# A third landing buffer for weight pieces in a fused attention and two-layer MLP kernel, paid for with one buffer of normalised outputs and one of early transposed halves

## The chip, the core and the metric

One core of a Trainium2 chip runs the whole program. Its engines are named as the profile names them: PE (TensorE, with its weight loads PEld), DVE (VectorE), ACT (ScalarE), POOL (GpSimd) and SP (SyncE, which here issues nearly all DMAs; its rows are marked SPq). The metric is the device time of one execution in microseconds, the median of several runs.

## What is computed

Two batches of eight heads of clustered attention (768 positions, head size 64), then two pairs of dense layers on the 1536 tokens:

```
q_n, k_n, c_n = normalised q, k, centroids
q_assign = argmax(q_n @ c_n.T)          # 16 clusters per head
k_assign = argmax(k_n @ c_n.T)
mask = q_assign[..., :, None] == k_assign[..., None, :]
scores = where(mask, q @ k.T / sqrt(64), -1e9)
attn = softmax(scores)                  # + 1e-9 in the sum
x = (attn @ v) as [1536, 512]
x = softplus(x @ w_in1) @ w_out1        # 512 -> 2048 -> 512
out = leaky_relu(x @ w_in2, 0.01) @ w_out2
```

## The kernel before

**Numbers.** Every float32 operand of a product is split into two float16 halves, a high part and the rest, so that a product costs three matmuls of halves. The weights lie in memory in float64, as pairs of 32-bit integers: DVE puts a float32 together from each pair with three integer operations (`decode`, lines 140, 143 and 146), ACT scales and rounds it to the high half (line 162), DVE writes the low half (line 163).

**A piece of weights.** `w_piece` (line 150) handles 128 rows of 512 numbers. It takes a tile `st` of 4 KB per partition from the pool `wst`, which has two buffers of it, issues its load on SP (line 153), and returns a function `conv` that decodes and splits the piece later. There are 32 such pieces, 16 of `w_in1` and 16 of `w_out1`; here they are called piece 0 to piece 31. `w_step` (in the main function) converts the piece loaded in the step before and loads the next one. The load is put on SP behind the transpose `tq` of a head two ahead of the one at work (`behind_tk`, with `wtie["h"]`), so SP's queue holds head h+2's `tq` first and then the pieces of head h. All 32 pieces are converted while the attention runs. The weights of the last two layers come later by functions of their own, which also take `st` from `wst`.

**A head of attention.** For each of the 16 heads in turn: `split` casts q and k to halves (ACT lines 293 and 295 into `nq` and `n1`, POOL line 294) and transposes `n1` by DMA into `t` (line 297, pool tag `t1`: the early halves, of which the scores are made). `assign_mm` (PE line 306) and `assign_el` (DVE lines 319 to 325, ACT lines 328 and 329) find the clusters and write them beside the halves in `nq`; this is transposed into `tq` (line 331). `emit_s1` (PE line 345, DVE line 352) computes scores once for the row maxima, `emit_m` (PE line 366, ACT line 374) writes the maxima into `tq`, `emit_s2` (PE lines 392 and 393, ACT line 399) computes the scores again and their exponentials, `emit_pv` (PE lines 415 to 433) multiplies with v, `emit_empty` (PE line 451) closes the sum, and `emit_norm` divides (DVE line 473 into `y`) and splits the result (ACT line 475, POOL line 476).

**Buffers.** `BUFS` gives for each tag a pair (late, early): buffers in the pool `at`, which lives through the attention, and further ones in `ep`, used by the first eight heads alone and given back at head 8. Before, `t1` has (4, 2) and `y` has (2, 0). A head's `t` is free again after its last matmul of line 393.

**What sets the order.** The program is written with a priority on each step (`at_pri`), and a scheduler places all instructions engine by engine, by priorities and by its own estimate of times; each engine then runs its own list strictly in that order, SP too. A wait at the head of an engine's list therefore holds everything behind it. From head 8 on, steps of the first dense layer (`layer_in`, PE line 697, 16 steps of 12 matmuls; its activation is on ACT lines 520 to 523) are mixed in, then steps of the second (`layer_mid`, PE line 710).

Of the kernel before, what the change touches and what calls it, by code (L numbers as in the profile page):

```python
# [11 lines left out]
I32 = mybir.dt.int32  # L12
# [10 lines left out]


BUFS = {
# [4 lines left out]
}  # L30
N_BUFS, V_BUFS = (2, 2), 3
PSUM_BUFS = {"as": 1, "s1": 2, "s2": 2}
# [11 lines left out]

FF_PRI, FF_STEP, FF_RATE = 8, 0.25, 0.75

W_FREE, W_FROM, W_TO, W_PER = 4, 8, 10, 5
W_PRI = ((0, 0.5), (17, 0.3))
W2_STEPS = 88
# [7 lines left out]
def attn_moe_kernel(  # L57
# [27 lines left out]
    wst = ctx.enter_context(tc.tile_pool(name="wst", bufs=2, side="right"))  # L85
# [6 lines left out]
    at = bctx.enter_context(tc.tile_pool(name="at", bufs=1, side="right", reuse_waits="tile"))  # L92
# [3 lines left out]
    turn = {}  # L96
# [41 lines left out]
    def decode(c, st):  # L138
        lo, hi = st[:, :, 0], st[:, :, 1]
        V.tensor_scalar(  # L140
            out=c, in0=hi, scalar1=3, scalar2=0x3FFFFFFF, op0=ALU.logical_shift_left, op1=ALU.bitwise_and
        )
        V.scalar_tensor_tensor(  # L143
            out=c, in0=hi, scalar=-0x40000000, in1=c, op0=ALU.bitwise_and, op1=ALU.bitwise_or
        )
        V.scalar_tensor_tensor(  # L146
            out=c, in0=lo, scalar=29, in1=c, op0=ALU.logical_shift_right, op1=ALU.bitwise_or
        )
        return c

    def w_piece(dsth, dstl, src):
        st = wst.tile([128, 512, 2], I32, tag="st", name="st")
        nc.sync.dma_start(out=st, in_=src.rearrange("p (n t) -> p n t", t=2))

        def conv(bank=False):
            if bank:
                c = pm.tile([128, 512], I32, tag="m0", name="wcp")
            else:
                c = wst.tile([128, 512], I32, tag="wc", name="wc")
            decode(c, st)  # L160
            cf = c.bitcast(F32)
            S.activation(out=dsth, in_=cf, func=AF.Copy, scale=WS)
            V.scalar_tensor_tensor(out=dstl, in0=cf, scalar=WS, in1=dsth, op0=ALU.mult, op1=ALU.subtract)

        return conv

    def in_pieces(w, wh, wl):
        wi = w.bitcast(I32)
        for f in range(DFF // 512):
            for kk in range(KDM):  # L170
                cs = slice(f * 512, (f + 1) * 512)
                src = wi[kk * 128:(kk + 1) * 128, f * 1024:(f + 1) * 1024]
                yield partial(w_piece, wh[:, kk, cs], wl[:, kk, cs], src)

    def out_pieces(w, wh, wl):
        wi = w.bitcast(I32)
        for kk in range(KFF):
            yield partial(w_piece, wh[:, kk, :], wl[:, kk, :], wi[kk * 128:(kk + 1) * 128, :])
# [738 lines left out]
    st = {"credit": 0.0}  # L917
# [83 lines left out]
```

## Time and profile before

| | us |
|---|---|
| median of 3 runs | 734.42 (733.02 to 736.55) |
| profiled execution | 732.15 |
| its span | 730.4 |
| PE busy in the span | 677.0 (93%) |
| DVE busy | 517.3 (71%) |
| ACT busy | 410.9 (56%) |
| POOL busy | 402.5 (55%) |

The attention takes the first 274 us and a little more; its last head ends inside the second dense layer. Busy time of PE is modelled at each instruction's end: matmuls overlap, so a busy share says that PE had matmuls in flight and not that it could take no more. What PE lost is read from idle times and from the distance between starts. DMA-issuing instructions are shown on SP from the moment they are issued; the time before, when SP waits for a buffer, is in the view of waits.

### The profile page before, as it was taken

How to read it: one execution, taken by the hardware profiler on the slowest of the kernel's cores; microseconds unless marked ns; L12 is line 12 of the kernel's file. 1: busy time of each engine (PE TensorE's matmuls, PEld its weight loads, DVE VectorE, ACT ScalarE, POOL GpSimd, SP SyncE). 2: the span in 40 equal slices, each digit the busy share in tenths (PEclk: the TensorE clock that was granted, in tenths of full speed). 3: DMA queues.
4: the chain of work that ended last, by engine and by line, in shares of the span. 5: the costliest groups of instructions: out<-in, count | busy, mean ns of one | idle time of the engine just before them, and what ended most of it. 6: DMA issues, size and time to landing. Idle time of an engine off the chain costs nothing. (4 is left out here: it accounts for less than half of the span.)

```text
span 730.4 us, 18968 instructions
## 1 busy us (share of the span) xinstructions
PE 677.0 (93%) x7584; PEld 506.7 (69%) x7584; DVE 517.3 (71%) x1167; ACT 410.9 (56%) x1087; POOL 402.5 (55%) x494
## 2 busy tenths in 40 slices
PE   1798899998889899999999999999999999999997
PEld 1367677665656566656666566558999999999996
DVE  4797798998898782069787867965585757575545
ACT  5476666768878753355245425526555555565553
POOL 6387777778888864303324233325556465565653
PEclk9999999999999999999999999999999999999999
DMA  8985966766565632013322355787000000000000
GB/s 204 221 173 113 181 136 122 170 123 173 129 161 152 141 116 53 2 35 103 110 93 82 108 175 193 235 304 261 3 31 2 30 2 7 27 2 31 2 31 30
DMA packets 104521, 77.87 MB, mean 107 GB/s; under 512 B 78320, under 2 KB 92656, under 8 KB 104432
## 3 DMA queue, kind: packets, MB, share of 16 engines
q1 hardware_dynamic: 104288, 76.40, 40.4%
q8 instruction: 59, 0.97, 0.5%
q14 instruction: 30, 0.25, 0.1%
q10 hardware_dynamic: 144, 0.26, 0.1%
HBM read 50.36 MB, written 10.49 MB: 83 GB/s over the span
## 5 line engine op out<-in xcount | busy, mean ns | idle before, releaser
L401 POOL TENSOR_TENSOR pl<-p 128x768 f16<-128x768 f32 x88 | 128.3, 1468 | 56.3 <-ACT p L399 36.0
L352 DVE TENSOR_REDUCE mm<-s 128x1 f32<-128x384 f32 x190 | 100.6, 548 | 19.3 <-PE s L345 16.7
L562 PEld LDWEIGHTS <-w_in2h 128*128 128x128 f16 x1344 | 98.2, 98 | 5.3 <-issue 0.7
L570 DVE TENSOR_TENSOR gl<-r,gh 128x384 f16<-128x384 f32 (+1 forms) x96 | 63.2, 659 | 50.0 <-ACT gh L608 49.3
L697 PE MATMUL m<-xt,w_inh 128*128 128x384 f16 x512 | 93.8, 326 | 4.2 <-ACT rl L521 3.4
L399 ACT ACTIVATE p<-s 128x384 f32<-128x384 f32 x160 | 74.2, 492 | 30.9 <-PE s L393 28.3
L710 PE MATMUL m<-g_l,w_outh 128*128 128x384 f16 x256 | 83.4, 326 | 2.0 <-DVE g_l L511 1.9
L710 PE MATMUL m<-g_h,w_outh 128*128 128x384 f16 x256 | 83.5, 326 | 0.0
L710 PE MATMUL m<-g_h,w_outl 128*128 128x384 f16 x256 | 83.3, 326 | 0.0
L570 POOL TENSOR_TENSOR r<-r,r 128x128 f32<-128x128 f32 x95 | 47.8, 520 | 55.5 <-ACT r L600 55.2
L697 PEld LDWEIGHTS <-w_inh 128*128 128x128 f16 x512 | 49.7, 98 | 38.7 <-issue 6.1
L608 ACT CAST gh<-r 128x384 f16<-128x384 f32 (+1 forms) x96 | 54.2, 565 | 36.6 <-POOL r L570 33.6
L710 PEld LDWEIGHTS <-w_outh 128*128 128x128 f16 x512 | 49.8, 98 | 32.5
L345 PE MATMUL s<-tq 128*128 128x384 f16 x190 | 62.0, 345 | 9.3 <-DMA tq<-nq 4.5
L562 PEld LDWEIGHTS <-gh 128*128 128x128 f16 x672 | 60.5, 98 | 6.4 <-issue 1.1
L200 POOL TENSOR_TENSOR wd<-wd 128x256 f32<-128x256 f32 x32 | 29.3, 925 | 53.9 <-DVE sg L194 39.2
L562 PE MATMUL i<-xt,w_in2h 128*128 128x128 f16 x576 | 57.2, 219 | 0.1
L392 PE MATMUL s<-t 128*128 128x384 f16 x160 | 53.2, 333 | 3.1 <-ACT p L399 2.3
L393 PE MATMUL s<-tq 128*128 128x384 f16 x160 | 53.2, 333 | 1.6 <-ACT tq L374 1.6
L562 PE MATMUL i<-sh,w_in2h 128*128 128x128 f16 x384 | 53.5, 219 | 0.4 <-ACT r L600 0.4
L562 PE MATMUL i<-sl,w_in2h 128*128 128x128 f16 x384 | 53.5, 219 | 0.0
L562 PE MATMUL i<-sh,w_in2l 128*128 128x128 f16 x384 | 53.4, 219 | 0.0
(145 smaller groups left out, 1861.1 us busy)
## 6 DMA issues: line engine op xcount, KB each, us to landing
st<-in_moe_w_in_dram SPq DMA_DIRECT2D x32, 512.0 KB, 4.6
st<-in_moe_w_out_dram SPq DMA_DIRECT2D x32, 512.0 KB, 3.7
kept<-sg SPq DMA_DIRECT2D x16, 256.0 KB, 2.8
qk<-in_q_dram SPq DMA_DIRECT2D x16, 192.0 KB, 3.5
qk<-in_k_dram SPq DMA_DIRECT2D x16, 192.0 KB, 3.7
v<-in_v_dram SPq DMA_DIRECT2D x16, 192.0 KB, 4.7
kept<-sg SPq DMA_DIRECT2D x24, 128.0 KB, 2.7
out_dram<-ob SPq DMA_DIRECT2D x11, 256.0 KB, 2.0
```

Of the source, the lines that this page charges most:

```text
L200: G.tensor_tensor(out=out, in0=in0, in1=in1, op=ALU.subtract)
L345: PE.matmul(out=o, lhsT=t[:, c, :], rhs=tk[:, 3 * j:3 * j + 3, :], start=True, stop=True,)
L352: V.reduce_max(out=mms[h % 2][:, c, j:j + 1], in_=bank[:, 0:3 * 128], axis=AX)
L392: PE.matmul(out=o, lhsT=t1[:, kt, 1, :], rhs=t1[:, 3 * j:3 * j + 3, 0, :], start=True, stop=False)
L393: PE.matmul(out=o, lhsT=t2[:, kt, :], rhs=tqh[:, 3 * j:3 * j + 3, :], start=False, stop=True)
L399: S.activation(out=p[:, j, :], in_=sp, func=AF.Exp, scale=scale)
L401: G.tensor_tensor(out=pl, in0=p, in1=pb, op=ALU.subtract)
L562: one = PE.matmul(out=bank, lhsT=w_, rhs=x_, start=(first and i == 0), stop=(i == len(ops) - 1), skip_group_check=True)
L570: eng.tensor_tensor(out=out, in0=in0, in1=in1, op=op)
L608: S.copy(out=gh[:, lo:hi], in_=r[:, lo:hi])
L697: PE.matmul(out=hp, lhsT=w_, rhs=x_, start=(i == 0), stop=(i == len(ops) - 1))
L710: PE.matmul(out=yp, lhsT=w_[:, kk, ms], rhs=g_[:, kk, :], start=(n == 0), stop=(n == 3 * KFF - 1))
```

## The change

`w_piece` takes its tile in turn from three buffers: two of `wst`, and a third with the same tag in the pool `at`, so it exists in the attention alone. The turn counts pieces, so each piece's tile follows from its number. To make room, `y` goes from two buffers to one, and the early part of `t1` from two to one. The late part stays at four. Nothing is computed differently.

```diff
-    "qk": (2, 1), "n1": (1, 2), "t1": (4, 2), "tq": (3, 1),
+    "qk": (2, 1), "n1": (1, 2), "t1": (4, 1), "tq": (3, 1),
...
-    "dd": (2, 0), "y": (2, 0), "xn": (2, 0),
+    "dd": (2, 0), "y": (1, 0), "xn": (2, 0),
...
+ST_MORE = 1
...
     def w_piece(dsth, dstl, src):
-        st = wst.tile([128, 512, 2], I32, tag="st", name="st")
+        n = turn["st"] = (turn.get("st", -1) + 1) % (2 + ST_MORE)
+        st = (wst if n < 2 else at).tile([128, 512, 2], I32, tag="st", name="st", bufs=2 if n < 2 else ST_MORE)
         nc.sync.dma_start(out=st, in_=src.rearrange("p (n t) -> p n t", t=2))
```

The numbers of instructions stay the same on every engine; the scheduler puts many of them elsewhere. Lines from 152 on stand two lower in the changed kernel, so line 297 there is 299. Three places matter below.

On SP, early in the attention: `t_1261`, `t_1561` and `t_1861` are the early halves of heads 5, 6 and 7, `nq_85` is the `tq` transpose of head 4, `st` a piece of weights. Before:

```order
L274 DMA qk<-in_k_dram 128x384
L297 DMA_TRANSPOSE t_1561<-n_1554 128x12x128
L273 DMA qk<-in_q_dram 128x384
L274 DMA qk<-in_k_dram 128x384
L297 DMA_TRANSPOSE t_1861<-n_1854 128x12x128
L331 DMA_TRANSPOSE tq<-nq_85 128x12x128
L153 DMA st<-in_moe_w_in_dram 128x1024
L280 DMA v_1_93<-in_v_dram 128x6x64
L273 DMA qk<-in_q_dram 128x384
L274 DMA qk<-in_k_dram 128x384
L331 DMA_TRANSPOSE tq<-nq_86 128x12x128
L153 DMA st<-in_moe_w_in_dram 128x1024
```

After:

```order
L299 DMA_TRANSPOSE t_1261<-n_1254 128x12x128
L275 DMA qk<-in_q_dram 128x384
L276 DMA qk<-in_k_dram 128x384
L299 DMA_TRANSPOSE t_1561<-n_1554 128x12x128
L333 DMA_TRANSPOSE tq<-nq_85 128x12x128
L155 DMA st<-in_moe_w_in_dram 128x1024
L282 DMA v_1_93<-in_v_dram 128x6x64
L275 DMA qk<-in_q_dram 128x384
L276 DMA qk<-in_k_dram 128x384
L299 DMA_TRANSPOSE t_1861<-n_1854 128x12x128
L333 DMA_TRANSPOSE tq<-nq_86 128x12x128
L155 DMA st<-in_moe_w_in_dram 128x1024
```

The early halves stand later among the `tq` transposes: head 7's now stands directly ahead of the `tq` of head 5 (`nq_86`), while the piece of weights stays directly behind its `tq`.

On SP, some 30 us later: `t_2469` is the early halves of head 9, `nq_88` and the following `nq_85` are the `tq` transposes of heads 7 and 8. Before:

```order
L297 DMA_TRANSPOSE t_2469<-n_2462 128x12x128
L331 DMA_TRANSPOSE tq<-nq_88 128x12x128
L153 DMA st<-in_moe_w_in_dram 128x1024
L280 DMA v_1_93<-in_v_dram 128x6x64
L454 DMA_TRANSPOSE xt_83<-xn 128x12x128
L153 DMA st<-in_moe_w_in_dram 128x1024
L331 DMA_TRANSPOSE tq<-nq_85 128x12x128
```

After:

```order
L333 DMA_TRANSPOSE tq<-nq_88 128x12x128
L155 DMA st<-in_moe_w_in_dram 128x1024 x2
L282 DMA v_1_93<-in_v_dram 128x6x64
L456 DMA_TRANSPOSE xt_83<-xn 128x12x128
L299 DMA_TRANSPOSE t_2469<-n_2462 128x12x128
L333 DMA_TRANSPOSE tq<-nq_85 128x12x128
```

Head 9's halves moved from ahead of head 7's `tq` to directly ahead of head 8's, and one piece of weights moved up by two places.

On PE, where the closing sum of head 12 has freed a `tq` buffer and the first scores of head 15 wait for its `tq`: behind the last scores before the dense layer's step, before:

```order
L393 LDWEIGHTS tq
L393 MATMUL s_5113<-tq 128x384
L697 LDWEIGHTS w_inh
L697 MATMUL m<-xt_83,w_inh 128x384
L697 LDWEIGHTS w_inh
L697 MATMUL m<-xt_83,w_inh 128x384
```

After:

```order
L395 MATMUL s_5113<-tq 128x384
L712 LDWEIGHTS w_outh
L712 MATMUL m<-g_h,w_outh 128x384
L712 LDWEIGHTS w_outh
L712 MATMUL m<-g_l,w_outh 128x384
L712 LDWEIGHTS w_outl
```

Before, 12 matmuls of line 697 follow here and then 17 small ones of `emit_pv`; now 23 of line 710 (712 there) and 6 small ones.

## Rows read from the trace of the kernel before

**Rows 1.** Busy by stretch: stretch, us, each engine's busy us, PE clock, DMA share, GB/s

```profile
37.00:150.00 113.00, 104.28 (x1547) 77.92 (x1545) 96.23 (x230) 77.71 (x192) 86.73 (x72) 1.00 0.74 152
150.00:274.00 124.00, 110.17 (x1361) 74.22 (x1360) 105.62 (x217) 93.59 (x227) 97.88 (x87) 0.99 0.58 140
```

**Rows 2.** Timeline of PE: start us, us, line, operation, [idle before, releaser]; back-to-back matmuls

```profile
41.89 0.19 PE L429 MATMUL x<-v,p 128*128 128x64 f16 x1
41.92 0.19 PE L428 MATMUL x<-v,p 128*128 128x65 f16 x1
...
47.66 0.32 PE L392 MATMUL m<-t 128*128 128x384 f16 x1
47.82 0.32 PE L345 MATMUL s<-tq 128*128 128x384 f16 x1
```

**Rows 3.** Waits of SP: line, releaser, us in total, times, longest us

```profile
SPq L153 <- DVE wcp L146: 35.0, 10, 5.6
```

**Rows 4.** Waits of DVE for pieces, whole run, and two of them in the timeline

```profile
DVE wcp L140 <- DMA st<-in_moe_w_in_dram: 7.2, 3, 3.2
...
61.79 0.69 DVE L140 TENSOR_SCALAR wcp<-st 128x512 int32<-128x512 int32 x1 [3.25 <-DMA st<-in_moe_w_in_dram]
...
166.97 0.69 DVE L140 TENSOR_SCALAR wcp<-st 128x512 int32<-128x512 int32 x1 [1.68 <-DMA st<-in_moe_w_in_dram]
```

**Rows 5.** Timeline of SP, the loads of those two pieces

```profile
55.23 1.50 SPq L331 DMA_TRANSPOSE tq<-nq  x1
56.82 0.86 SPq L153 DMA_DIRECT2D st<-in_moe_w_in_dram  x1
...
161.83 1.45 SPq L153 DMA_DIRECT2D st<-in_moe_w_in_dram  x2
```

**Rows 6.** Timeline of POOL and DVE, two heads' normalised outputs

```profile
55.68 0.92 POOL L476 TENSOR_TENSOR xn<-y,xn 128x384 f16<-128x384 f32 x1
...
66.33 0.56 DVE L473 TENSOR_TENSOR y<-x,dd 128x384 f32<-128x384 f32 x1
```

**Rows 7.** Timeline of ACT, SP and PE around the tq of head 5

```profile
70.09 0.27 ACT L329 ACTIVATE nq<-oh 128x96 f16<-128x96 f16 x1
...
70.38 1.46 SPq L331 DMA_TRANSPOSE tq<-nq  x1
...
71.43 0.33 PE L393 MATMUL m<-tq 128*128 128x384 f16 x1
...
75.43 0.92 ACT L293 CAST nq<-qk 128x384 f16<-128x384 f32 x2 [2.80 <-DMA tq<-nq]
...
76.90 0.32 PE L393 MATMUL m<-tq 128*128 128x384 f16 x1 [1.77 <-ACT tq L374]
```

**Rows 8.** Timeline of PE and SP around the tq of head 8

```profile
106.20 0.33 PE L393 MATMUL m<-tq 128*128 128x384 f16 x1
...
107.67 1.45 SPq L331 DMA_TRANSPOSE tq<-nq  x1
...
114.80 0.32 PE L393 MATMUL m<-tq 128*128 128x384 f16 x1 [0.20 <-ACT tq L374]
```

**Rows 9.** Instructions of line 297 on SP: count, ns min/median/max, first and last start

```profile
L297 SPq DMA_TRANSPOSE t<-n x16: 1438/2060/3711, 7.9 to 216.3; - x16
```

**Rows 10.** Timeline of PE, waits for transposes of heads 11, 13, 14, then tq

```profile
143.81 0.53 PE L306 MATMUL as<-ct,t 128*128 128x16 f16 x15 [0.63 <-DMA t<-n]
...
182.08 0.48 PE L306 MATMUL as<-ct,t 128*128 128x16 f16 x13 [1.22 <-DMA t<-n]
...
199.87 0.56 PE L306 MATMUL as<-ct,t 128*128 128x16 f16 x16 [0.61 <-DMA t<-n]
...
209.21 0.50 PE L345 MATMUL s<-tq 128*128 128x384 f16 x2 [0.35 <-DMA tq<-nq]
...
250.18 0.50 PE L345 MATMUL s<-tq 128*128 128x384 f16 x2 [1.92 <-DMA tq<-nq]
```

**Rows 11.** Waits of PE between 40 and 290 us, the dense layer's steps

```profile
PE m L697 <- ACT rl L521: 3.4, 8, 0.7
```

## The prediction, made before the changed kernel ran

> **What bounds the kernel now.** I read four views: busy time by stretch, the waits of each engine, the timelines around those waits, and the planned order of both kernels. From 37 to 274 us, where the attention runs, no engine is alone the limit: of 113 us up to 150, PE has matmuls in flight for 104.3, DVE works for 96.2, POOL for 86.7; from 150 to 274 the four are at 110, 106, 94 and 98 of 124 [rows 1]. PE's share overstates it: a matmul of 384 columns is shown for 0.32 us, but the next starts 0.16 us later, and the small ones of `emit_pv` start every 0.03 us [rows 2]. So I work with idle time on PE, and price PE work at 0.16 and 0.03 us each. PE runs its list strictly in order; a transpose or a cast that comes late holds it, and such places decide what the change is worth.
>
> **The third piece buffer, by itself.** SP stands 35.0 us in ten waits before issuing a piece, because the conversion still reads the buffer [rows 3]. That looks like the gain, but SP's waiting costs only if somebody waits for what is queued behind. The direct sufferer is DVE: it waits for pieces three times, 7.2 us in all, 3.25 and 1.68 us of it at 61.79 and 166.97 us [rows 4]; the first wait, 7.2 - 3.25 - 1.68 = 2.3 us, is that for the very first piece, which no buffer can advance. The two others I follow to SP. The piece of 61.79 was issued at 56.82, right behind the `tq` of 55.23, and the piece of 166.97 at 161.83, likewise behind a `tq` [rows 5]. There was no wait for a buffer between: a piece is tied behind the `tq` of a head, and the new order shows the same tie, `tq`, then `st`. A third buffer lets later pieces move up by one or two places and leaves these two where they are. I take 0 us, with -5 us (3.25 + 1.68) as the end if both went.
>
> **One buffer of `y`.** POOL's last reading of `y` ends at 55.68 + 0.92 = 56.60; the next head writes it at 66.33 [rows 6]. Ten microseconds lie between: 0 us. If the next division came right behind, the cost would be a wait of up to 0.92 us a head on DVE; nothing in the trace comes near.
>
> **One buffer less of early halves, heads 5 to 9.** The halves of heads 5 to 8 now take over the buffer of the head five before, where it was six, and head 9 that of head 5. Their consumers come late enough: counted in the new order at the prices above, 10 us of PE work or more lie between the buffer's last reading and the assignment of heads 5 to 8, and 4.7 us at head 9, which I cost at nothing as well. The cost lies on SP. The transpose of head 7 now waits for the last scores of head 2, and it stands directly ahead of the `tq` of head 5; that of head 9 waits for head 5's, directly ahead of the `tq` of head 8. The `tq` of head 5 had no slack: its last input was written at 70.09 + 0.27 = 70.36, it was issued at 70.38; ACT waited 2.80 us for it before it could go on to the maxima of head 3, and PE 1.77 us for these at 76.90 [rows 7]. Issuing one transpose takes SP 1.44 to 3.71 us, median 2.06 [rows 9].
> - At head 5's `tq`: the last scores of head 2 end at 71.43 + 0.33 = 71.76 [rows 7]. In the new order 57 of the 576 matmuls ahead of them have moved behind: 3 of 384 columns, 48 small ones and 6 in float32, which I price at four small ones: 0.5 + 1.4 + 0.7 = 2.6 us. DVE's list up to the assignment of head 5 is as long as before (139 instructions). So the buffer comes free between 69.2 and 71.8, and `tq` can go 2.06 us later, 71.2 to 73.8: 0.8 to 3.4 us late. I take 1.1, nearer to the early end, since PE's list is what really moved.
> - At head 8's `tq`: head 5's last scores end at 106.20 + 0.33 = 106.53; with 2.06 us of issue, `tq` goes at 108.6 in place of 107.67: 0.9 us late. PE's wait at 114.80 was 0.20 us [rows 8], so the path is just as tight. Ends 0.3 (1.44 us of issue) and 2.6 (3.71).
>
> Together +2.0 us, between 0 (other engines' waits absorb it) and +6.0.
>
> **What moves in the second half.** From head 10 on the buffers are those of before, but the scheduler put other work between "buffer free" and "needed". I count it in both orders, against PE's idle at these places [rows 10]. Head 11's assignment gets 13 matmuls of 384 columns and 78 small ones more cover: 4.4 us, so its 0.63 us goes. Head 13's loses 4 large ones, so its 1.22 grows by 0.64. Head 14's gains one large and loses 18 small: its 0.61 grows by 0.38. The first scores of head 13 get 12 small ones more, and 0.35 us goes. Those of head 15 get 23 matmuls of line 710 in place of 12 of line 697 and lose 11 small ones: 11 x 0.16 - 11 x 0.03 = 1.4 of the 1.92 us goes. Sum: -0.63 + 0.64 + 0.38 - 0.35 - 1.4 = -1.4 us, with ends -2.9 (all three gains in full, no growth) and +1.0 (the two growths alone). The dense layer's steps stand closer together at first and wider apart later; PE's waits for their activation are 3.4 us in eight [rows 11], and I let them move by 1 us either way, 0 as the value.
>
> **The sum.** 0 + 0 + 2.0 - 1.4 + 0 = +0.6 us on the profiled execution: 732.15 + 0.6 = 732.8. That execution stands 2.27 us under the median of the runs, 734.42, which by the same step becomes 735.0. The bounds of the terms give 734.4 - 2.9 - 1 = 730.5 and 734.4 + 6.0 + 1 + 1 = 742.4.
>
> **Rival 1: the loads were the limit after all (faster).** If the third buffer lets the scheduler's order run ahead in earnest, DVE's two waits vanish and with them what hangs on DVE's list, the row maxima and the cluster search. Price: -4.9, and with the -1.4 of the second half 734.4 - 6.3 = 728. For it speaks that the waits of SP repeat ten times and DVE is busy for 96.2 of 113 us [rows 1]; against it, that both waits were released by a load behind a `tq`. It is decided by whether the wait at 61.79 us shrinks. The Trainium skill ("Perfetto Trace Analysis", section "Optimization Strategy") would have it this way: a gap that repeats on the engine that should be saturated can mean that there is no memory for the next tile. The trace agrees by half: the gap that repeats is SP's [rows 3], and SP is not the engine to be saturated.
>
> **Rival 2: the early halves block SP (slower).** If the last scores of head 2 do not come earlier, the `tq` of head 5 is late by the full wait and issue, 71.76 + 2.06 - 70.38 = 3.4 us, and that of head 8 by 106.53 + 3.71 - 107.67 = 2.6; with the growth at heads 13 and 14 of 1.0 and nothing gained elsewhere, 734.4 + 7.0 = 741.4. It decides as soon as head 2's last scores end later than head 5's cluster marks are written. For it speaks that SP's `tq` had no slack in the trace; against it, the 57 matmuls moved behind.
>
> **Rival 3: nothing reaches the chip's time.** The buffer is there and lies unused, and the late `tq` is caught up: 734.4, inside the forecast's class.
>
> **How the numbers follow.** Forecast together with rival 3: 0.54; rival 1: 0.20; rival 2: 0.26. A measurement of this kernel can tell about 0.5%, 3.7 us, from no change, so 735.0 is "the same". The forecast alone reaches from 730.5 to 739; 8 in 10 needs a part of both rivals: 728.5 to 741. Faster by over 0.5% (under 730.7): rival 1 and a little of the forecast's low end, 0.22; slower (over 738.1): most of rival 2, 0.25; the same: 0.53.
>
> **What would show it.** In the profile after: DVE's waits for pieces still near 7 us, two of them behind a `tq`; SP's wait for the conversion well under 35 us with no engine the better for it; the `tq` of heads 5 and 8 issued right behind a transpose of line 299, with ACT's wait before the next maxima longer than 2.8 us; PE's idle before the first scores of head 15 about 0.5 us. If DVE waits under 3 us for pieces, rival 1 is right; if ACT waits over 5 us behind the `tq` of head 5, rival 2.

## The result, and the profile after

The changed kernel takes 740.78 us (median of six runs, 738.96 to 741.96) against 734.1 us of the kernel before (six runs, 733.02 to 736.55). The ratio is 1.0094, with a 95% interval of 1.0072 to 1.0116: slower by 0.94%, 6.7 us by the medians. The forecast was 735.0, no change; the time lies just inside its range of 728.5 to 741, but the forecast of no change is wrong, since the whole interval lies above 1. The profiled execution is the slowest of its six, 741.96 us with a span of 740.2; that of before, 732.15 us, lies below all six of its own. So the two traces differ by 9.8 us where the medians differ by 6.7, and the traces serve below to find places, the medians for sizes.

Busy by stretch in the changed kernel, with the columns of [rows 1]:

```profile
37.00:150.00 113.00, 99.38 (x1437) 73.70 (x1435) 89.34 (x210) 72.13 (x179) 79.86 (x65) 0.97 0.64 131
150.00:274.00 124.00, 110.35 (x1360) 73.44 (x1356) 104.17 (x217) 93.51 (x229) 98.68 (x88) 0.97 0.62 149
```

From 37 to 150 us every engine got less done than in [rows 1]: PE 1437 instructions in place of 1547, DVE 210 in place of 230. From 150 to 274 us PE got through as many as before (1360 and 1361). The loss arises in the early heads. The last matmul of head 7's sum starts at 152.1 us in this trace and at 142.4 in that of before, the last of head 15's at 321.9 and 313.5; so most of what is lost by head 7 is still lost at the end (in between the distance grows, to 16.2 us at head 11, and shrinks again).

The pieces, in the waits of the whole run and then in the timeline of DVE:

```profile
DVE wcp L141 <- DMA st<-in_moe_w_in_dram: 8.2, 4, 3.0
SPq L155 <- DVE wcp L147: 29.4, 10, 5.1
```

```profile
61.44 0.69 DVE L141 TENSOR_SCALAR wcp<-st 128x512 int32<-128x512 int32 x1 [3.00 <-DMA st<-in_moe_w_in_dram]
...
151.36 0.70 DVE L141 TENSOR_SCALAR wcp<-st 128x512 int32<-128x512 int32 x1 [1.42 <-DMA st<-in_moe_w_in_dram]
```

DVE waits as long for pieces as in [rows 4], 8.2 us after 7.2, and the wait at 61 us is still there. SP, in the second row, waits 29.4 us for the conversion where it waited 35.0 [rows 3].

Now the place at which the prediction looked for a price, the `tq` of head 5 (engines SP, ACT and PE in order of time):

```profile
67.29 0.33 PE L395 MATMUL m<-tq 128*128 128x384 f16 x1
...
67.49 1.47 SPq L299 DMA_TRANSPOSE t<-n  x1
...
69.43 0.49 ACT L401 ACTIVATE p<-m 128x384 f32<-128x384 f32 x1
...
69.97 0.28 ACT L331 ACTIVATE nq<-oh 128x96 f16<-128x96 f16 x1
...
70.28 1.43 SPq L333 DMA_TRANSPOSE tq<-nq  x1
...
72.98 0.50 PE L368 MATMUL s<-ident,dg 128*128 128x128 f16 x6
...
75.69 0.92 ACT L295 CAST nq<-qk 128x384 f16<-128x384 f32 x2 [5.44 <-DMA tq<-nq]
76.64 0.21 ACT L446 CAST h<-as 32x65 f16<-32x65 f32 x1
76.76 0.85 ACT L376 CAST tq<-s 32x384 f16<-32x384 f32 x2
...
77.28 0.32 PE L395 MATMUL m<-tq 128*128 128x384 f16 x1 [2.92 <-ACT tq L376]
...
77.76 0.20 PE L308 MATMUL as<-ct,t 128*128 128x16 f16 x2
...
85.64 1.44 SPq L333 DMA_TRANSPOSE tq<-nq  x1
```

The first row is the last of head 2's scores. The half of head 7 (its early halves, line 299) goes directly ahead of `tq`, at 67.49, but `tq` itself goes at 70.28, no later than the 70.38 of [rows 7]. What has grown is ACT's wait behind it: 5.44 us in place of 2.80. The same stretch of ACT in the kernel before shows why, with PE's assignment of head 6 and SP's `tq` of that head behind it:

```profile
70.42 0.49 ACT L399 ACTIVATE p<-s 128x384 f32<-128x384 f32 x1
71.53 0.49 ACT L399 ACTIVATE p<-s 128x384 f32<-128x384 f32 x1 [0.61 <-PE s L393]
71.91 0.49 ACT L399 ACTIVATE p<-m 128x384 f32<-128x384 f32 x1
72.42 0.21 ACT L444 CAST h<-as 32x65 f16<-32x65 f32 x1
...
73.49 0.70 PE L306 MATMUL as<-ct,t 128*128 128x16 f16 x22
...
81.69 2.49 SPq L331 DMA_TRANSPOSE tq<-nq  x1
```

Before, three exponentials of head 2 and the copy of `emit_sv` (sums over v, which PE leaves in the PSUM bank `as`; ACT line 444) stood between head 5's marks and the casts of head 9, which wait for that `tq` since they overwrite the `nq` that it reads. In the changed kernel head 2's scores come earlier, their exponentials stand ahead of the marks (the last at 69.43), and the casts of head 9 are the very next thing on ACT. Behind them stand the copy of `emit_sv`, now at 76.64 in place of 72.42, and the copies of head 3's maxima, 0.38 us later than before (76.76 after 76.38). The copy of `emit_sv` also frees the one bank `as`, which head 6's assignment writes next; that assignment moves from 73.49 to 77.76, the `tq` of head 6 from 81.69 to 85.64. Two more such places follow. At head 4 (SP, ACT, PE):

```profile
88.82 3.35 SPq L299 DMA_TRANSPOSE t<-n  x1
...
95.75 0.93 ACT L297 COPY n<-nq 128x384 f16<-128x384 f16 x2 [1.86 <-DMA t<-n]
96.58 0.48 ACT L401 ACTIVATE p<-m 128x384 f32<-128x384 f32 x1
...
97.12 0.32 PE L394 MATMUL m<-t 128*128 128x384 f16 x1 [1.98 <-ACT p L401]
```

The half of head 8 goes at 88.82 (before: 78.2), ACT's copies for head 9 wait for it in front of head 4's exponentials, and PE waits for these. And at the `tq` of head 8:

```profile
112.71 1.44 SPq L299 DMA_TRANSPOSE t<-n  x1
...
114.25 1.97 SPq L333 DMA_TRANSPOSE tq<-nq  x1
...
119.51 0.93 ACT L295 CAST nq<-qk 128x384 f16<-128x384 f32 x2 [2.59 <-DMA tq<-nq]
122.39 0.52 ACT L287 CAST v<-v 128x384 f16<-128x384 f32 x1 [1.13 <-DMA v<-in_v_dram]
...
123.45 0.48 PE L395 MATMUL m<-tq 128*128 128x384 f16 x1 [2.46 <-ACT tq L376]
```

Head 8's marks are written at 112.62 + 0.30 = 112.92, so the half ahead of it makes this `tq` 1.3 us late; the rest of the 6.6 us by which it stands behind [rows 8] has come down the chain. The Trainium skill ("PSUM — Partial Sum Buffer", section "Engine vs sequencer instructions") calls the queue of ScalarE strictly first in, first out. The trace agrees: head 3's maxima were multiplied out on PE by 73.5 us (72.98 + 0.50) and their copies still started at 76.76, behind the casts that waited.

### The profile page after: what moved, and what is told of

The parts are those of the page before. It is cut to its first block, busy times and chain, and to the rows that moved or that the text cites. A ratio compares the mean times of both kernels' runs of the same rounds, so it can differ in the third digit from the quotient of the medians.

```text
span 740.2 us, 18961 instructions
## 1 busy us (share of the span) xinstructions
PE 680.1 (92%) x7584; PEld 507.0 (68%) x7584; DVE 517.4 (70%) x1167; ACT 411.1 (56%) x1087; POOL 401.8 (54%) x494
```

## The experiments

All ratios are against the kernel before, run beside it on the same chip, with 95% intervals. PE's matmuls "at another place" are counted by going through the lists of two traces side by side, by line and tile; each list has 7584. The theories of the expectations are told with the groups in which they were set up.

### One part at a time

Three parts can carry the loss: the cut of the early halves, through the order that the scheduler then writes (theory A) or through SP's waits for a half's buffer (theory B), or the third piece buffer (theory C).

**The cut alone** (`e1_cut`):

```diff
-    "qk": (2, 1), "n1": (1, 2), "t1": (4, 2), "tq": (3, 1),
+    "qk": (2, 1), "n1": (1, 2), "t1": (4, 1), "tq": (3, 1),
```

> Only the buffers of early halves go from six to five (4 late, 1 early); two piece buffers and two of y as before. Its instructions stand in the order of the changed kernel up to head 9. Theory A (the loss comes with the cut of the halves, through the order that follows from it): 740 to 741 us. Theory B (the loss comes with the cut, through SP waiting for a half's buffer in front of the cluster marks): 740 to 741 us too. Theory C (the loss comes with the third piece buffer, whose loads collide with other transfers): 734 to 735 us.

739.91 us, ratio 1.0103 (1.0070 to 1.0135): the whole loss.

**The third buffer alone** (`e2_third`), laid into a part of the resident weights that is filled last, so that nothing has to be cut for it:

```diff
+ST_UNTIL = 27
...
-        st = wst.tile([128, 512, 2], I32, tag="st", name="st")
+        n = turn["st"] = turn.get("st", -1) + 1
+        if n % 3 == 2 and n < ST_UNTIL:
+            st = w_outl[:, 12:16, :].rearrange("p k f -> p (k f)").bitcast(I32).rearrange("p (n t) -> p n t", t=2)
+        else:
+            st = wst.tile([128, 512, 2], I32, tag="st", name="st")
```

> Only the third piece buffer, with nothing cut: every third piece up to the 27th is loaded into the part of the resident w_outl that is filled last. Six buffers of early halves, two of y. Theories A and B: no change within 2 us of 734, since the order up to head 9 is that of the kernel before and DVE's two waits for pieces stay. Theory C: 740 us.

735.58 us, ratio 1.0035 (1.0010 to 1.0059). Not the 740 us of theory C, but not quite nothing either; `e15_third_moved` comes back to it.

**One `y` alone** (`e11_y_alone`; `"y": (1, 0)` and nothing else):

> One buffer of y in place of two and nothing else; every instruction stands where it stood. All theories: 732 to 735.5 us, no change, as ten microseconds lie between the last reading of y and its next writing.

732.04 us, ratio 0.9990 (0.9967 to 1.0013): nothing.

### Order or waits

To part the order from the waits, a table imposes the list of one kernel on another. For every engine it ties each instruction behind the one that stands ahead of it in the list to be copied; this sets the order of issue and nothing else:

```diff
+    found = {i.name: i for i in nc.cur_bb.bb.instructions}
+    for packed in ORDER.values():
+        row = zlib.decompress(base64.b85decode(packed)).decode().split()
...
+        for first, then in zip(row, row[1:]):
+            tc.add_manual_dep(
+                found[then], first,
...
```

**The changed kernel's order on the buffers of before** (`e3_order_of_after`):

> All buffers as before (six halves, two pieces, two y), but every instruction of every engine queue in the order of the changed kernel, imposed by a table. So no wait for a missing buffer can arise, and what is left is the order. Theory A: the whole loss, 740 to 741 us. Theory B: 734 to 736 us.

783.45 us, ratio 1.0690 (1.0662 to 1.0719): nobody's expectation. Up to head 7 it runs as the changed kernel does (the last matmul of head 7's sum starts at 150.7 us). Behind that the list counts on three piece buffers and has two, as its waits show:

```profile
SPq L155 <- DVE wcp L148: 78.7, 17, 8.4
...
PE as L308 <- DMA t<-n: 34.5, 6, 11.8
```

SP stands 78.7 us before pieces, with transposes of halves queued behind, and PE waits for these halves, 34.5 us in six waits (one of them, 11.8, is the first of the program). So this run can't tell A from B in its total; `e5` repeats it with the list of the cut alone, which has two piece buffers.

**The cut's order on the buffers of before** (`e5_order_of_cut`):

> All buffers as before (six halves, two pieces, two y), every instruction of every engine queue in the order of the kernel with the cut alone. Theory A (the order that follows from the cut costs, not the waits themselves): the loss of the cut alone, 739 to 742 us. Theory B (SP's waits for a half's buffer cost): 732 to 735 us, as no half waits for a buffer any more.

738.87 us, ratio 1.0061 (1.0035 to 1.0087). No half waits for a buffer here, and 0.61 of the 1.03% of the cut are still there. Theory A carries most of it; B is left with about 0.4%, which the intervals don't separate from zero.

**PE's list of before on the changed kernel** (`e4_pe_of_before`):

> The changed kernel (five halves, three pieces, one y) with PE's list alone put back into the order of the kernel before by a table; the other engines' lists come out as the scheduler then finds them (the half of head 7 then stands behind the cluster marks of head 5, not ahead). Theory A, if PE's list is what matters: 734 to 737 us. Theory B: 740 us or more, since the halves' buffers are as scarce as in the changed kernel.

738.55 us, ratio 1.0085 (1.0055 to 1.0116). Putting PE's list back is no cure, so the order that costs is not PE's alone. The reverse of `e5`, all lists of before on five halves, was not run.

**SP's list of the cut on the buffers of before** (`e6_sp_of_cut`; the other lists as the scheduler then writes them):

> All buffers as before, SP's list alone in the order of the kernel with the cut (the half of head 5 behind the cluster marks of head 3, 7 behind 4, 8 behind 6, 9 behind 7); the other lists as the scheduler then writes them. Theory A: 737 to 742 us, since the late halves carry the rest of the order with them. Theory B: 732 to 735 us. Theory D (it is PE's and ACT's lists, not SP's): 732 to 735 us.

731.29 us, ratio 0.9979 (0.9959 to 1.0000). The late halves on SP cost nothing by themselves, so theory A in the form "late halves" falls, and theory D is left: what costs is in the other lists. This is by exclusion, as the scheduler wrote those anew here too (1973 of PE's matmuls stand at another place than before).

### Is any other order as bad?

Rival R: the numbers of the kernel before were chosen with its own order, and any other loses. Two kernels with all buffers of before and as much moved on PE (2763 and 2391 matmuls at another place than before, 2370 with the cut).

```diff
-W_PRI = ((0, 0.5), (17, 0.3))
+W_PRI = ((0.3, 0.5), (17, 0.3))
```

> The kernel before with the priority of the weight pieces 0.3 heads later and nothing else: as many positions of PE's list change as with the cut, but of the halves only that of head 7 falls behind a cluster mark transpose that it stood ahead of. Theory A: 732 to 736 us. Rival R (any other order than the one that the numbers of the kernel before were chosen for costs as much): 737 to 742 us.

732.20 us, ratio 0.9993 (0.9966 to 1.0021).

```diff
-LEAD_SPLIT, LEAD_ASSIGN, LEAD_MAX, LEAD_M, LEAD_LOAD, LEAD_NORM = 2.5, 2, 4, 2.5, 2, 4
+LEAD_SPLIT, LEAD_ASSIGN, LEAD_MAX, LEAD_M, LEAD_LOAD, LEAD_NORM = 2, 2, 4, 2.5, 2, 4
```

> The kernel before with the lead of the splitting reduced from 2.5 to 2 heads and nothing else: as many positions of PE's list change as with the cut, yet no half of heads 5 to 9 falls behind a cluster mark transpose that it stood ahead of, but for that of head 8, which moves ahead of one more. Theory A: 732 to 736 us. Rival R: 737 to 742 us.

733.22 us, ratio 0.9997 (0.9976 to 1.0017). Both as fast as before: R falls. It is something particular in the order of the cut.

### The two waits of ACT

Theory E: the loss sits where ACT waits at the head of its list, in front of head 3's maxima and of head 4's exponentials. Theory F: it is spread. `e9_changed_mended` moves these two pieces of ACT's list in the changed kernel:

```diff
-            S.copy(out=n_[:, t_, :, 0:D], in_=qk[:, t_])
+            with behind(done[3] if h == 9 else None):
+                S.copy(out=n_[:, t_, :, 0:D], in_=qk[:, t_])
...
-            S.copy(out=n1[:, :, 3 * t_, :], in_=n_[:, t_, :, 0:D])
+            with behind(ex[4, 4] if h == 9 else None):
+                S.copy(out=n1[:, :, 3 * t_, :], in_=n_[:, t_, :, 0:D])
```

Here `done[3]` is the last copy of head 3's maxima, `ex[4, 4]` an exponential of head 4, and `behind` ties the issue order.

> The changed kernel with two pieces of ACT's list moved and nothing else: the casts of q and k of head 9 stand behind the copies of head 3's maxima (they wait 5.44 us for the cluster marks of head 5 in the changed kernel, with the copies queued behind), and the copies for its half behind the ninth exponential of head 4 (they wait 1.86 us for the half of head 8). Theory E (these two waits of ACT are where the new order costs): PE's 3.09 us at head 3 and 2.13 us at head 4 go for the most part, 735 to 737.5 us. Theory F (the loss is spread over the order, or is the late halves themselves): 739 us or more.

736.51 us, ratio 1.0040 (1.0016 to 1.0064): 0.54 of the 0.94% are gone, 4.0 us. Against the changed kernel only 180 of PE's matmuls stand elsewhere, all of them among the first 970, so this is a small edit in effect too. Its timeline at head 3 (ACT, PE, SP), ACT at head 4, and PE behind the `tq` of head 8:

```profile
69.62 0.28 ACT L338 ACTIVATE nq<-oh 128x96 f16<-128x96 f16 x1
72.83 0.21 ACT L453 CAST h<-as 32x65 f16<-32x65 f32 x1 [2.92 <-PE as L449]
73.00 0.85 ACT L383 CAST tq<-s 32x384 f16<-32x384 f32 x2
75.32 0.93 ACT L301 CAST nq<-qk 128x384 f16<-128x384 f32 x2 [1.48 <-DMA tq<-nq]
...
76.81 0.32 PE L401 MATMUL m<-t 128*128 128x384 f16 x1 [0.61 <-ACT p L408]
...
81.53 1.44 SPq L340 DMA_TRANSPOSE tq<-nq  x1
...
93.98 0.93 ACT L304 COPY n<-nq 128x384 f16<-128x384 f16 x2
...
119.40 0.48 PE L402 MATMUL m<-tq 128*128 128x384 f16 x1 [2.31 <-ACT tq L383]
```

The copies stand at 72.83 and 73.00, as soon as PE has delivered; PE's 2.92 us have become 0.61, the `tq` of head 6 is back at 81.53, and the copies at head 4 no longer wait. The gain arises at the first place: the last matmul of head 4's sum starts at 104.9 us in place of 108.3, and of the second place PE has little, since it waits 0.50 us for an exponential at 90.13 and 1.16 us for POOL at 95.94 where it waited 1.98 us for ACT. The two moves were not run apart. The third place of the changed kernel was not touched: PE still waits 2.31 us at 119.40, after 2.46.

**The same move in the kernel before** (`e10_before_same_move`; head 9's first casts alone):

> The kernel before with the casts of q and k of head 9 behind the copies of head 3's maxima and nothing else. PE waits 1.9 us there in the kernel before. Theory E: 0.5 to 2 us faster than before, 732 to 733.5 us by the median of 733.6. Theory F: no change, 733 to 735 us.

728.26 us, ratio 0.9962 (0.9936 to 0.9988): faster than before, by 0.38%. ACT and PE at the place of [rows 7]:

```profile
73.78 0.85 ACT L381 CAST tq<-s 32x384 f16<-32x384 f32 x2 [0.72 <-PE s L373]
75.61 0.92 ACT L299 CAST nq<-qk 128x384 f16<-128x384 f32 x2 [0.99 <-DMA tq<-nq]
...
79.42 0.32 PE L399 MATMUL m<-t 128*128 128x384 f16 x1 [0.80 <-ACT p L406]
```

The copies of the maxima go at 73.78 instead of 76.38, and PE's 1.77 us before them are gone. But the gain can't be put down to this wait. The scheduler answers the tie with another order: 2291 of PE's matmuls stand at another place than before, where `e9` had 180. And the trace is soon no longer ahead: the last matmul of head 4's sum starts at 103.1 us (before: 103.0), that of head 7's at 144.3 (142.4). Only from 150 us on does PE get through more, 1425 instructions against the 1361 of [rows 1]:

```profile
150.00:274.00 124.00, 112.22 (x1425) 74.86 (x1422) 107.33 (x224) 99.19 (x240) 103.64 (x92) 1.00 0.64 155
```

So the gain is larger than theory E expected (0.5 to 2 us), and it is not shown that the wait brings it; where the 0.38% comes from stays open. With its two piece buffers and six halves this kernel has the lowest median of this study.

**The move for heads 7 to 11** in the kernel before (`e12_before_all_heads`; `done[h - 6] if 6 < h < 12 else None`):

> The kernel before with the casts of q and k of heads 7 to 11 each behind the copies of the maxima six heads before. Theory E: as the move for head 9 alone or better, 730 to 733.5 us. Theory F: no change or slower, 733 to 737 us, as the halves come later by it.

734.04 us, ratio 1.0014 (0.9995 to 1.0034): as a rule for all heads the move gains nothing. This tie too rewrites the order (2626 of PE's matmuls), so it does not tell which head would lose by the move.

### What the move leaves

0.40% remain in `e9`. Theory G: the halves' own waits. Theory H: the third piece buffer. `e13_cut_mended` is the cut alone with the two moves of `e9`, `e14_mended_order_free` its order on six halves, `e15_third_moved` the third buffer of `e2` with the move of `e10`.

> The cut of the halves alone, with the two moves on ACT of the mended changed kernel; two piece buffers, two of y. Its order is that of the mended changed kernel up to head 9. Theory G (what the mend leaves, 0.4%, is the halves' own waits for a buffer): 735 to 737 us. Theory H (what is left belongs to the third piece buffer, which alone cost 0.35%): 732 to 734 us.

737.46 us, ratio 1.0024 (0.9997 to 1.0051).

> All buffers as before (six halves), every instruction of every engine queue in the order of the kernel with the cut and the two moves. Theory G: 2 to 4 us faster than the same order with five halves, 731 to 734 us. Theory H: as long as the same order with five halves, within 1 us.

734.11 us, ratio 0.9990 (0.9961 to 1.0020).

> The third piece buffer alone (in the resident w_outl) with the casts of head 9 behind the maxima of head 3, to be held against the same move without the third buffer (728.3 us). Theory H: 730 to 732 us, the third buffer costs 2 to 3 us again. Theory G: 728 to 730 us.

733.84 us, ratio 0.9988 (0.9959 to 1.0016).

The strongest reading is `e14` against `e5`. Both have the buffers of before, and both run the cut's order; they differ by the two moved pieces and 180 places of PE's list. The ratio goes from 1.0061 (1.0035 to 1.0087) to 0.9990 (0.9961 to 1.0020), intervals that don't meet. The traces show it early: the last matmul of head 4's sum starts at 109.4 us in `e5` and 102.3 in `e14`, that of head 15's at 319.8 and 312.7. Of these 7.1 us 2.3 stand there already at head 1's sum (62.9 and 60.6), ahead of the first place that differs, so the traces put 4.8 us down to the move. By the medians the cost of the order, 0.61%, goes with the two pieces of ACT's list.

Same order, five or six halves: 0.34% between `e13` and `e14`, as the 0.42% between `e1` and `e5`. Each pair of intervals overlaps, so a cost of the waits of some 3 us is likely and not settled. The traces show a place for it, on SP. With five halves:

```profile
53.01 1.94 SPq L304 DMA_TRANSPOSE t<-n  x1
55.04 1.46 SPq L338 DMA_TRANSPOSE tq<-nq  x1
```

and with six:

```profile
45.91 1.93 SPq L299 DMA_TRANSPOSE t<-n  x1
...
52.40 1.45 SPq L333 DMA_TRANSPOSE tq<-nq  x1
```

The half of head 6 waits until 53.01 for head 1's last scores and holds the `tq` of head 4 behind it, which goes 2.6 us later than with six halves; 1.1 us of this are head 4's marks, written later too (53.46 after 52.38). It is what the prediction described, one head earlier than it put it. In the kernel before the half of head 7 had stood at that place and held the same `tq` until 55.2 us, so this is no loss against before.

Theory H: the third buffer costs 0.26% in `e15` against `e10` and 0.35% in `e2`, each with overlapping intervals or nearly so, and nothing in the changed kernel itself (1.0094 with it, 1.0103 without). `e15` and `e10` also differ in the order (1398 of PE's matmuls), so its own price stays open, between nothing and some 0.35%.

A third candidate for what is left in `e9` was not run: the wait behind the `tq` of head 8, 2.31 us of PE in `e9`, 2.46 in the changed kernel and 0.20 before [rows 8]. As at head 3, pieces that wait stand there ahead of the copies of the maxima on ACT: the casts that wait for the `tq`, and a cast of v that waits for its load (0.94 us in `e9`).

## Why the prediction failed, step by step

**The third buffer, 0 us.** In the changed kernel right: DVE's waits for pieces stayed, 8.2 after 7.2 us, because the pieces still go behind a `tq`. Nothing was gained; alone it measured 0.35% (2.6 us) slower, which the term of 0 did not have. SP's wait for the conversion was to fall "well under 35" and fell only to 29.4. The rival that made the loads the limit is out: its deciding sign, the wait at 61.79 us, went from 3.25 to 3.00.

**One `y`, 0 us.** Right, by `e11`.

**The early halves, +2.0 us (0 to +6.0).** This is the step that failed: the cut alone costs 1.03%, 7.6 us on 734, above the term's upper end. It priced a late `tq` on SP. At head 5 the +1.1 was wrong, since head 2's last scores ended at 67.6 us (67.29 + 0.33), before the range of 69.2 to 71.8 that I had counted out, and `tq` was not late at all; at head 8 the +0.9 was about right (1.3). What I had left out is the rest of the order. I counted PE's and DVE's lists up to the places where halves are needed, found cover there, and costed "the consumers come late enough" at nothing. They came late because the scheduler had moved them, and with them it had moved ACT's exponentials out of the gap between head 5's marks and the casts of head 9. That gap was in [rows 7]: ACT's wait of 2.80 us, with the maxima behind it. I read it as the price of a late `tq`; it is as well the price of lost cover in front of it, and a look at ACT's list there would have shown that the cover was gone. `e5` shows the order alone to cost 0.61%, `e14` that this cost goes when two pieces of ACT's list are moved, and `e9` that the same two are worth 0.54% in the changed kernel, most of it by the trace at head 3. What is left, 0.40%, has candidates (SP's waits for a half's buffer, the wait behind the `tq` of head 8) and no proof.

**The second half, -1.4 us (-2.9 to +1.0).** The waits of PE in the changed kernel that answer to [rows 10]:

```profile
192.25 0.41 PE L308 MATMUL as<-ct,t 128*128 128x16 f16 x10 [0.70 <-DMA t<-n]
...
214.22 0.71 PE L308 MATMUL as<-ct,t 128*128 128x16 f16 x22 [0.98 <-DMA t<-n]
222.84 0.50 PE L347 MATMUL s<-tq 128*128 128x384 f16 x2 [0.27 <-DMA tq<-nq]
```

Head 11's 0.63 us and the 1.92 us before head 15's first scores are gone, head 14's wait grew from 0.61 to 0.98 as worked out (0.99), head 13's fell to 0.70 instead of growing. Sum: -0.63 - 0.52 + 0.37 - 0.08 - 1.92 = -2.8 us, inside the bounds. Between the sums of heads 7 and 15 the trace made up 9.7 - 8.4 = 1.3 us. This step held in sign, though in between the distance first grew to 16.2 us, for which the prediction had no term; the dense layer's waits, 3.1 us after 3.4 [rows 11], did too.

**Rival 2, slower, 741.4 us.** It had the time, almost, and its sign came true: ACT waited 5.44 us behind the `tq` of head 5. Its mechanism did not: that `tq` was on time. The sign was badly chosen, since a wait grows when its end comes later or when the work ahead of it goes away. The time of issue, 70.28, would have told the two apart. The condition I gave it (head 2's last scores later than the marks) was not met either.

**The chances.** The 0.26 for rival 2 stood on one mechanism with one price. That a buffer less makes the scheduler write other lists on all engines was seen and counted on two of them; no case was set up for what it does on ACT. That the measured 740.78 still lies inside the range, by 0.2 us, is luck: the range's upper end came from rival 2's late `tq`, which did not happen.

## What to carry to other kernels

A buffer taken away where a scheduler orders the work cost here first through the new order and only then, if at all, through its waits; compare the lists of all engines around each place that was tight before, above all what now stands between a producer and the wait for it, and what stands behind that wait. A wait at the head of an in-order list is cheap as long as it has cover ahead and nothing urgent behind: where a trace shows the second, move the piece that waits behind what is urgent, there and not by rule (for five heads at once the same move gained nothing). Count what else such a tie moves before its gain is put down to it: here 180 matmuls in one kernel and 2291 in the other. And imposing one kernel's order on another's buffers parts order from waits, if the list was made for buffers that are there (`e5`, and not `e3`).

## What the runs showed of the hardware that was not expected

The granted clock of PE fell at a place of the changed kernel where it had not before, but this does not go with the change. The stretch behind PE's wait at 77 us, in the changed kernel, in the cut alone (`e1`) and in the mended kernel (`e9`), and the same place in `e11`, which runs the order of before; columns as in [rows 1]:

```profile
77.20:82.20 5.00, 4.92 (x50) 3.01 (x50) 2.78 (x7) 3.08 (x8) 2.34 (x2) 0.67 0.29 61
```

```profile
77.20:82.20 5.00, 5.00 (x74) 3.64 (x73) 4.08 (x11) 4.08 (x10) 3.78 (x4) 1.00 0.21 47
```

```profile
77.20:82.20 5.00, 4.88 (x51) 3.56 (x50) 3.03 (x10) 4.27 (x12) 4.91 (x4) 1.00 0.27 57
```

```profile
76.00:80.00 4.00, 3.72 (x22) 2.04 (x22) 1.01 (x4) 2.98 (x7) 2.24 (x2) 0.59 1.23 206
```

0.67 means that about two thirds of the stretch ran at 1.2 GHz and the rest at 2.4. PE had waited 2.92 us just before; in the cut alone it had waited nearly as long and kept the full clock, so the wait by itself doesn't settle it; and in `e11`, whose order is that of before, the clock fell there too (0.59). At most 5.0 x 0.33 = 1.7 us of full-speed work are lost in this stretch, if PE was the limit there. The mean clock of a whole run is a little lower in the changed kernel, 0.987 over its six runs after 0.991 over 29 runs of the kernel before, and a small part of the loss may go with it. It is not what the loss is made of: `e4` has 0.992 and loses 0.85%, `e14` has 0.988 and loses nothing.

An order made for three piece buffers and run with two cost 6.9% (`e3`), more than seven times the change under study. PE waits 34.5 us for halves in it, 14.0 in the changed kernel.
